# Row maxima in a clustered-attention and mixture-of-experts kernel: full-length passes over two thirds of the queries replaced by a maximum from PSUM and folds over all queries

## The chip, the cores and the metric

One NeuronCore of one Trainium2 chip. The metric is the device time of one execution in microseconds (us); lower is better. Three executions of the kernel before took 465.91, 466.88 and 467.42 us, median 466.88 us.

## What is computed

Two stages on one core. First an attention with a cluster mask: 2 batches, 8 heads, 768 tokens, 64 values per head. Every query and every key is assigned to the nearest of 16 centroids of its head (by cosine), and a query sees only keys of its own cluster:

```python
mask = q_assign[:, :, :, None] == k_assign[:, :, None, :]
scores = np.where(mask, scale * (q @ k.T), -1e9)
scores = scores - np.max(scores, axis=-1, keepdims=True)
attn = np.exp(scores) / (np.sum(np.exp(scores)) + 1e-9)
out = attn @ v
```

Then a mixture of 8 experts on the 2 x 768 tokens of 512 values that come out of it: a router picks one expert per token (a token can also keep the expert of the token before it), and the expert is two products with a relu between them, `p[e] * (relu(x @ w1[e]) @ w2[e])`.

The row maximum, `np.max(scores, axis=-1)`, is the part that the change edits.

## The kernel before, in words

The 16 (batch, head) combinations are handled one after the other; two heads of one batch make a pair u. For each head the kernel needs the 768 x 768 masked scores twice. The first time (function `stC`, queries on partitions) serves only to find each query's maximum. The maximum then goes as an extra column into the tile Q2, which one DMA transposes into Q2T (`fin`), and the second time (function `stD`, keys on partitions) the score product takes it off by itself, so that ScalarE can exponentiate the PSUM tile at once (L360, tile `e`, 32-bit). The exponentials are used as a 16-bit upper half and a 16-bit remainder `lo`; the remainder is a subtraction of two SBUF operands, seven times a head on GpSimd (L365) and twice on VectorE (L371). Products with the values follow (L388 to L390), then the division (`nm1`, L399 to L402; `nm2`, L410 on GpSimd).

A head's row-maximum stage consists of nine units. A unit is two matmuls (L318) that make a PSUM tile of 2 query tiles of 128 x 256 keys: `qp` is the pair of query tiles (0 to 2) and `kc` the third of the keys (0 to 2). `UORD` gives the order of the nine. There are two PSUM buffers for these tiles. In the kernel before,

- units with qp of 0 or 1 (two thirds of the queries) are copied by ScalarE as 16-bit data into the SBUF tile `ev` (L321), 128 x 512 each, six a head;
- units with qp of 2 are reduced by VectorE straight from PSUM into `mx` (L323), three a head;
- the four rows of `ev`, 768 keys each, are passed over by VectorE with an instruction that multiplies by 1 and gathers the maximum in its accumulator (L330; the profile shows it as TENSOR_SCALAR_CACHE_REDUCE and a DVE_READ_ACCUMULATOR);
- `fin` joins the three partial maxima of the last third (L336), writes them to Q2 (L338, L339) and issues the transposing DMA on SP's queue (L340).

The order of the work is written out by hand in one loop over steps `n` (L1114). In each step it emits one unit of the row maxima, 16 steps ahead (`c = n + LEAD`), one score tile, the pieces of the row maxima that are due by the table `OFFS`, the VectorE remainder and the value product of earlier tiles, and then whatever other tasks are due: loads, splits into 16-bit halves (L207, L213, L223) and cluster assignment (L252 to L267) of later pairs, routing, and the splits of the first expert's weights (L859, L861). Nine steps make a head. The entries of `OFFS` are (steps after the head's first unit, piece): pieces 0 to 3 are the passes over `ev`, piece 4 is `fin`:

```python
for off, what in OFFS:
    m = c - (off if c > 10 else min(off, 8))
    if 0 <= m < 9 * NH and m % 9 == 0:
        if what < 4:
            cs_[m // 9][1][what]()
        else:
            ins = cs_.pop(m // 9)[2]().ins
```

A scheduler turns this into each engine's own in-order queue, with the order of emission as priority, and sets the semaphores. The first batch's routing and the first expert's products run inside the later heads; the other experts follow after attention.

Of the kernel before, what the change touches and what calls it, by code (L numbers as in the profile page):

```python
# [36 lines left out]
NEQ = 2  # L37
NEM = 99
UORD = [(0, 0), (0, 1), (2, 0), (0, 2), (1, 0), (2, 1), (1, 1), (1, 2), (2, 2)]
OFFS = ((4, 0), (9, 1), (9, 2), (9, 3), (9, 4))  # L40
# [26 lines left out]
def tile_kernel(ctx, tc, q, k, v, centroids, w_gate, w_local, w1, w2, out):  # L67
# [43 lines left out]
    # constants  # L111
# [187 lines left out]
    # row maxima of head g: most units leave PSUM through ScalarE and are reduced as 16-bit data  # L299
    def stC(g):  # L300
# [3 lines left out]
        NEV = NEQ + (g % NEM == NEM - 1)  # L304
        NQ = 2 * NEV

        def unit(n):
            qp, kc = order[n]

            def f():  # L310
                if n == 0:
                    st["m"] = smp.tile([128, T], F32, name="m", tag="m", bufs=3)
                    st["mx"] = smp.tile([128, T, 3], F32, name="mx3", tag="mx3", bufs=3)
                    st["ev"] = smp.tile([128, 2 * NEV, 768], BF16, name="ev", tag="ev", bufs=EVB)
# [5 lines left out]
                if qp < NEV:  # L320
                    A.activation(out=st["ev"][:, 2 * qp:2 * qp + 2, kc * 256:kc * 256 + 256], in_=ps, func=AF.Copy)  # L321
                else:
                    mark["V"] = V.tensor_reduce(out=st["mx"][:, 2 * qp:2 * qp + 2, kc], in_=ps, axis=AX.X, op=ALU.max).ins  # L323
            return f

        def tree(i):
            e = st["ev"]
            for j in ((0, 1), (2, 3), (4, 5), ())[i]:
                if j < 2 * NEV:
                    mark["V"] = V.tensor_scalar(out=e[:, j], in0=e[:, j], scalar1=1.0, scalar2=None, op0=ALU.mult, op1=ALU.max, accum_out=st["m"][:, j:j + 1]).ins  # L330

        def fin():
            m = st["m"]
            q2 = rg(Q2, u)[:, hh]
            if NEV < 3:
                V.tensor_reduce(out=m[:, 2 * NEV:T], in_=st["mx"][:, 2 * NEV:T], axis=AX.X, op=ALU.max)  # L336
# [4 lines left out]
        return [unit(n) for n in range(9)], [lambda i=i: tree(i) for i in range(4)] if NQ else [], fin  # L341
# [226 lines left out]
    def lead(psp):  # L568
# [18 lines left out]
        # the first CAP_A of them come first, the rest with those of the next batch  # L587
# [8 lines left out]
    def unslot(pt, p, n, nm):  # L596
        """token indices of slots (0 where the slot is empty) for the gather and the scatter"""
# [17 lines left out]
    def lead_index(b, psp, tag=TX):  # L615
        """place of the leading expert's tokens of batch b, from 1; 0 for the others"""
# [46 lines left out]
    def plan(psp, tag):  # L663
        """ranks of the experts by their number of tokens, and each token's slot"""
# [20 lines left out]
        # index of each token among its expert's, its place in the block and the block  # L685
# [23 lines left out]
        # slot table: (place, block) <- token  # L709
# [23 lines left out]
        def over():  # L733
            """the slot table of the tokens past the static capacities, and the expert of each of its blocks"""
            c9 = tmp("c9", [128, E, E])
            n8 = tmp("n8", [128, E])
            # the key holds the number of tokens exactly
# [19 lines left out]
            # first block past the capacity, and capacity, of each token's expert  # L757
# [20 lines left out]
            # a token within the capacity has no block here  # L778
# [38 lines left out]
    def prio(d):  # L817
        """trace with a priority later by d"""
# [9 lines left out]
    def wload(r, kind, reg):  # L828
        """the loads and splits of the r-th expert's w1 (kind 0) or w2 (kind 1): pairs of steps"""
# [35 lines left out]
    def slot_blocks(cap):  # L865
        """blocks of slots: full ones of 128, whose output comes token-major, and a rest of up to 191"""
        nf = cap // 128
        if 0 < cap - nf * 128 < 64 and nf:
            nf -= 1
        return nf, cap - nf * 128  # L870
# [9 lines left out]
    def expert(r, cap, src, gi, sci, pr, mp, nbuf, g1pool=None, last=False, gates=None, putm=None):  # L880
        """gather, products and scatter of `cap` slots; gi, sci, pr give block i's column"""
        st = {"t": 0.0}

        def gate(t):
            """the next t us of this expert's products wait their turn behind the routing of the other batch"""
# [375 lines left out]
```

## Time and profile before

| | |
|---|---|
| median of three executions | 466.88 us |
| profiled execution: span from first to last instruction | 463.1 us |
| what lies around the span, by the three executions | 2.8 to 4.3 us |
| VectorE busy | 359.7 us, 78% |
| TensorE busy | 372.7 us, 80% |
| ScalarE busy | 264.6 us, 57% |
| GpSimd busy | 195.1 us, 42% |

In the profile PE is TensorE, DVE is VectorE, ACT is ScalarE, POOL is GpSimd and SP is SyncE. L330 is line 330 of the kernel before. A row of a list of instructions reads: line, engine, operation, tile written <- tiles read, shapes (partitions x elements and type), number of them | busy us in all, mean ns of one | idle us of the engine just before them, and what ended that idle time. Attention fills the span up to about 275 us, the experts the rest. Busy shares over the whole span mix these stages, so they are to be read stage by stage.

### The profile page before, as it was taken

To read this page: it belongs to the slowest core of one execution; us is meant where nothing else is said; L and a number is where in the kernel's file an instruction comes from. 1 tells how busy PE (TensorE), PEld (TensorE's weight loads), DVE (VectorE), ACT (ScalarE), POOL (GpSimd) and SP (SyncE) were. 2 spreads that over 40 slices of the span, in tenths; PEclk is the share of its full clock that TensorE was granted. 3 is DMA by queue.
4 is the path that set the end of the run, shared out by engine and by line. 5 is a ranking of instruction groups with operands and counts; after the bars stand their busy time and mean duration, and the time that the engine had idled before them with its cause. 6 is when DMAs were issued, how large, how long until landed. Compare 5 with 4: busy or idle time off the path is not lost. (4 is left out here: it accounts for less than half of the span.)

```text
span 463.1 us, 13303 instructions
## 1 busy us (share of the span) xinstructions
PE 372.7 (80%) x5315; PEld 315.7 (68%) x5315; DVE 359.7 (78%) x872; ACT 264.6 (57%) x493; POOL 195.1 (42%) x192
## 2 busy tenths in 40 slices
PE   0267697779788887988776699699999799999991
PEld 0246586668667775777665597498798597897870
DVE  7789999898989999989999338676685666566630
ACT  4277467667567875766776340145573765566430
POOL 3005447385647665656767631503233132201121
PEclk9998899898989999899999599899999899999997
DMA  8889889967967957237654601999699699697501
GB/s 191 120 192 205 248 124 223 213 134 178 171 154 159 152 116 119 47 82 147 151 169 128 124 8 33 259 282 245 194 347 324 191 313 314 212 281 240 183 31 33
DMA packets 125215, 81.48 MB, mean 176 GB/s; under 512 B 94537, under 2 KB 110153, under 8 KB 125152
## 3 DMA queue, kind: packets, MB, share of 16 engines
q1 hardware_dynamic: 122448, 73.47, 67.5%
q0 software_dynamic: 2704, 7.15, 4.4%
q8 instruction: 42, 0.69, 0.6%
q14 instruction: 21, 0.17, 0.1%
HBM read 47.04 MB, written 8.63 MB: 120 GB/s over the span
## 5 line engine op out<-in xcount | busy, mean ns | idle before, releaser
L365 POOL TENSOR_TENSOR lo<-e 128x512 f16<-128x512 f32 x112 | 129.1, 1171 | 97.3 <-ACT e L360 96.5
L360 ACT ACTIVATE e<-pst 128x512 f32<-128x512 f32 x144 | 82.1, 603 | 22.4 <-PE pst L358 18.4
L861 DVE SCALAR_TENSOR_TENSOR W<-wst,W 128x1024 f16<-128x1024 f32 x64 | 79.9, 1255 | 17.6 <-ACT W L859 17.4
L390 PE MATMUL o<-VH,lo 128*128 128x65 f16 x576 | 72.2, 197 | 16.9 <-DVE lo L371 15.8
L358 PE MATMUL pst<-Q2T,K2T 128*128 128x256 f16 x288 | 72.4, 289 | 7.5 <-DMA Q2T<-Q 7.5
L915 PE MATMUL g<-XT,W 128*128 128x200 f16 (+8 forms) x288 | 71.4, 259 | 7.5 <-DVE H L919 4.7
L357 PE MATMUL pst<-Q1T,K1T 128*128 128x256 f16 x288 | 76.0, 286 | 0.1
L318 PE MATMUL pm<-K2T,QMT 128*128 128x256 f16 x288 | 55.5, 291 | 23.5 <-DVE mx L323 18.1
L389 PE MATMUL o<-VL,e 128*128 128x64 f16 x576 | 74.4, 196 | 0.0
L388 PE MATMUL o<-VH,e 128*128 128x65 f16 x576 | 73.9, 198 | 0.0
L321 ACT ACTIVATE ev<-pm 128x512 bf16<-128x512 f32 x96 | 56.0, 599 | 28.2 <-PE pm L318 27.6
L916 PE MATMUL g<-XT,W 128*128 128x200 f16 (+8 forms) x288 | 71.5, 260 | 0.0
L859 ACT ACTIVATE W<-wst 128x1024 f16<-128x1024 f32 x64 | 66.9, 1052 | 5.8 <-DMA wst<-in_moe_w_dram 5.7
L390 PEld LDWEIGHTS <-lo 128*128 128x128 f16 x576 | 55.2, 100 | 22.1 <-DVE lo L371 19.2
L917 PE MATMUL g<-XT,W 128*128 128x200 f16 (+8 forms) x288 | 69.8, 260 | 0.0
L330 DVE TENSOR_SCALAR_CACHE_REDUCE ev<-ev 128x768 bf16<-128x768 bf16 x64 | 58.1, 943 | 0.1
L388 PEld LDWEIGHTS <-e 128*128 128x128 bf16 x576 | 55.5, 100 | 2.1 <-issue 0.2
L389 PEld LDWEIGHTS <-e 128*128 128x128 bf16 x576 | 55.5, 101 | 1.6
L918 ACT ACTIVATE H<-g 128x200 f16<-128x200 f32 (+8 forms) x72 | 24.3, 344 | 55.7 <-PE g L917 54.1
L919 DVE SCALAR_TENSOR_TENSOR H<-g,H 128x200 f16<-128x200 f32 (+8 forms) x72 | 25.9, 373 | 30.9 <-ACT H L918 30.3
L926 POOL DMA_INDIRECT out_dram<-ob,scim x16 | 18.3, 1146 | 71.0 <-ACT ob L924 30.5
L318 PEld LDWEIGHTS <-QMT 128*128 128x128 f16 x288 | 24.2, 103 | 30.4 <-issue 22.5
(298 smaller groups left out, 900.8 us busy)
## 6 DMA issues: line engine op xcount, KB each, us to landing
wst<-in_moe_w_dram SPq DMA_DIRECT2D x64, 512.0 KB, 5.4
xd<-xt SPq DMA_DIRECT2D x12, 384.0 KB, 3.6
ld_k<-in_k_dram SPq DMA_DIRECT2D x7, 384.0 KB, 4.7
ld_q<-in_q_dram SPq DMA_DIRECT2D x7, 384.0 KB, 5.0
ld_v<-in_v_dram SPq DMA_DIRECT2D x7, 384.0 KB, 4.5
Q1T<-QXT SPq DMA_DIRECT2D x14, 192.0 KB, 4.2
ld_k<-in_k_dram SPq DMA_DIRECT2D x2, 192.0 KB, 2.3
ld_q<-in_q_dram SPq DMA_DIRECT2D x2, 192.0 KB, 2.4
```

What stands on the lines that cost most here:

```text
L318: PE.matmul(out=ps[:, i], lhsT=rg(QMT, u)[:, hh * T + 2 * qp + i, :], rhs=rg(K2T, u)[:, hh * T + 2 * kc:hh * T + 2 * kc + 2, :], start=Tru ...
L357: PE.matmul(out=ps[:, i], lhsT=rg(K1T, u)[:, j, :], rhs=rg(Q1T, u)[:, hh * T + 2 * qc:hh * T + 2 * qc + 2, :], start=True, stop=False)
L358: PE.matmul(out=ps[:, i], lhsT=rg(K2T, u)[:, j, :], rhs=rg(Q2T, g)[:, 2 * qc:2 * qc + 2, :], start=False, stop=True)
L360: mark["A"] = A.activation(out=e, in_=ps.rearrange("p a b -> p (a b)"), func=AF.Exp, scale=SCL).ins
L365: G.tensor_tensor(out=lo, in0=e, in1=eh, op=ALU.subtract)
L388: PE.matmul(out=o[:, t, 0:65], lhsT=eh[:, sl], rhs=vh[:, hh, j, 0:65], start=first, stop=False, skip_group_check=True)
L389: PE.matmul(out=o[:, t, 0:64], lhsT=eh[:, sl], rhs=vl[:, hh, j, :], start=False, stop=False, skip_group_check=True)
L390: PE.matmul(out=o[:, t, 0:65], lhsT=lo[:, sl], rhs=vh[:, hh, j, 0:65], start=False, stop=False, skip_group_check=True)
L861: V.scalar_tensor_tensor(out=l[:, cs], in0=s[:, cs], scalar=WS, in1=h[:, cs], op0=ALU.mult, op1=ALU.subtract)
L915: PE.matmul(out=ps, lhsT=lh, rhs=XT[:, 2 * kk, 0:cap], start=(kk == 0), stop=False)
L916: PE.matmul(out=ps, lhsT=lh, rhs=XT[:, 2 * kk + 1, 0:cap], start=False, stop=False)
L917: PE.matmul(out=ps, lhsT=ll, rhs=XT[:, 2 * kk, 0:cap], start=False, stop=(kk == KD - 1))
```

## The change

All queries are now treated alike. ScalarE copies the units of the first two thirds of the keys (kc of 0 and 1) for all six query tiles into `ev`, which becomes 6 x 512 values in place of 4 x 768. A unit of the last third (kc of 2) is not reduced: VectorE takes, element by element, the maximum of its PSUM tile and of the copied first third, and writes it over that third in `ev`. Then `ev` is folded in halves by three element-wise maxima of two SBUF operands, 512 to 256 to 128 to 64 values a row, and one reduction of 6 x 64 values gives all six maxima. `mx` and the join of its parts are gone. The pieces are emitted 9, 10, 11 and 12 steps after the head's first unit, where half of the passes were emitted 4 steps after it and the other half 10; `fin` stays at 13. The order of the units stays, so that VectorE's units are now those at places 3, 7 and 8 of nine (counted from 0), where they were 2, 5 and 8.

```diff
-NEQ = 2
-NEM = 99
-OFFS = ((4, 0), (9, 1), (9, 2), (9, 3), (9, 4))
+OFFS = ((9, 0), (9, 1), (9, 2), (9, 3), (9, 4))
...
-                    st["mx"] = smp.tile([128, T, 3], F32, name="mx3", tag="mx3", bufs=3)
-                    st["ev"] = smp.tile([128, 2 * NEV, 768], BF16, name="ev", tag="ev", bufs=EVB)
+                    st["ev"] = smp.tile([128, T, 512], BF16, name="ev", tag="ev", bufs=EVB)
...
-                if qp < NEV:
-                    A.activation(out=st["ev"][:, 2 * qp:2 * qp + 2, kc * 256:kc * 256 + 256], in_=ps, func=AF.Copy)
+                ev = st["ev"][:, 2 * qp:2 * qp + 2]
+                if kc < 2:
+                    A.activation(out=ev[:, :, kc * 256:kc * 256 + 256], in_=ps, func=AF.Copy)
                 else:
-                    mark["V"] = V.tensor_reduce(out=st["mx"][:, 2 * qp:2 * qp + 2, kc], in_=ps, axis=AX.X, op=ALU.max).ins
+                    mark["V"] = V.tensor_tensor(out=ev[:, :, 0:256], in0=ps, in1=ev[:, :, 0:256], op=ALU.max).ins
             return f

-        def tree(i):
+        def fold(w):
             e = st["ev"]
-            for j in ((0, 1), (2, 3), (4, 5), ())[i]:
-                if j < 2 * NEV:
-                    mark["V"] = V.tensor_scalar(out=e[:, j], in0=e[:, j], scalar1=1.0, scalar2=None, op0=ALU.mult, op1=ALU.max, accum_out=st["m"][:, j:j + 1]).ins
+            mark["V"] = V.tensor_tensor(out=e[:, :, 0:w], in0=e[:, :, 0:w], in1=e[:, :, w:2 * w], op=ALU.max).ins
+
+        def last():
+            mark["V"] = V.tensor_reduce(out=st["m"], in_=st["ev"][:, :, 0:64], axis=AX.X, op=ALU.max).ins

         def fin():
...
-            if NEV < 3:
-                V.tensor_reduce(out=m[:, 2 * NEV:T], in_=st["mx"][:, 2 * NEV:T], axis=AX.X, op=ALU.max)
...
-        return [unit(n) for n in range(9)], [lambda i=i: tree(i) for i in range(4)] if NQ else [], fin
+        return [unit(n) for n in range(9)], [lambda: fold(256), lambda: fold(128), lambda: fold(64), last], fin
```

In both kernels the order of the units (qp, kc) is

```python
UORD = [(0, 0), (0, 1), (2, 0), (0, 2), (1, 0), (2, 1), (1, 1), (1, 2), (2, 2)]
```

## Rows read from the trace of the kernel before

**Rows 1.** The head of the profile's page: span, and of each engine busy us, share of the span and number of instructions.

```profile
span 463.1 us, 13303 instructions
...
PE 372.7 (80%) x5315; PEld 315.7 (68%) x5315; DVE 359.7 (78%) x872; ACT 264.6 (57%) x493; POOL 195.1 (42%) x192
```

**Rows 2.** Busy time by stretch. Columns: the stretch, its length, busy us and number of instructions of PE, PEld, DVE, ACT and POOL, granted TensorE clock, share of the DMA engines, GB/s.

```profile
67.00:239.00 172.00, 141.58 (x2375) 120.38 (x2372) 162.30 (x358) 120.93 (x238) 109.56 (x95) 0.96 0.73 149
...
239.00:275.00 36.00, 27.64 (x424) 23.54 (x421) 22.63 (x60) 17.28 (x33) 21.93 (x20) 0.86 0.37 87
```

**Rows 3.** VectorE's instructions in the stretch from 67 to 239 us, grouped by line and shape, costliest first.

```profile
L330 DVE TENSOR_SCALAR_CACHE_REDUCE ev<-ev 128x768 bf16<-128x768 bf16 x48 | 43.5, 943 | 0.1
L323 DVE TENSOR_REDUCE mx<-pm 128x2 f32<-128x512 f32 x37 | 25.3, 683 | 4.5 <-PE pm L318 4.4
L371 DVE TENSOR_TENSOR lo<-e 128x512 f16<-128x512 f32 x24 | 23.6, 984 | 0.1
...
L207 DVE SCALAR_TENSOR_TENSOR K<-ld_k,K 128x384 f16<-128x384 f32 x8 | 6.9, 894 | 0.0
L207 DVE SCALAR_TENSOR_TENSOR QX<-ld_q,QX 128x384 f16<-128x384 f32 x8 | 6.6, 868 | 0.1
L207 DVE SCALAR_TENSOR_TENSOR VL<-ld_v,VH 128x384 f16<-128x384 f32 x9 | 6.4, 709 | 0.0
L861 DVE SCALAR_TENSOR_TENSOR W<-wst,W 128x1024 f16<-128x1024 f32 x4 | 6.0, 1528 | 0.0
...
L259 DVE TENSOR_TENSOR eq<-eq,iota 128x384 f16<-128x384 f16 x5 | 3.7, 740 | 0.0
L267 DVE TENSOR_TENSOR oh<-eq,gm 128x384 f16<-128x384 f16 x5 | 3.6, 714 | 0.0
...
L213 DVE COPY QM<-QX 128x768 f16<-128x768 f16 x5 | 3.0, 593 | 0.0
L213 DVE COPY K<-K 128x768 f16<-128x768 f16 x5 | 2.8, 553 | 0.8 <-DMA K2T<-K 0.8
...
L223 DVE COPY Q<-QX 128x768 f16<-128x768 f16 x5 | 2.6, 526 | 1.6 <-DMA Q2T<-Q 1.6
...
L336 DVE TENSOR_REDUCE m<-mx 128x2 f32<-128x6 f32 x12 | 1.8, 150 | 0.1
```

**Rows 4.** GpSimd's instructions in the same stretch, grouped in the same way.

```profile
L365 POOL TENSOR_TENSOR lo<-e 128x512 f16<-128x512 f32 x83 | 97.1, 1188 | 50.5 <-ACT e L360 49.9 <-DVE m L336 0.4
L410 POOL TENSOR_TENSOR xt<-xf,xt 128x384 f16<-128x384 f32 x12 | 13.0, 1080 | 11.8 <-ACT xt L406 11.8
```

**Rows 5.** Who waited for whom in the same stretch: engine, tile and line that waited <- what it waited for: us in all, times, longest us.

```profile
PE pm L318 <- DVE mx L323: 11.2, 13, 2.6
...
DVE mx L323 <- PE pm L318: 4.4, 6, 1.3
```

**Rows 6.** VectorE's instructions in order of time from 146 to 149 us: start us, duration us, engine, line, operation, tiles and shapes.

```profile
146.30 0.94 DVE L330 TENSOR_SCALAR_CACHE_REDUCE ev<-ev 128x768 bf16<-128x768 bf16 x1
...
147.17 0.94 DVE L330 TENSOR_SCALAR_CACHE_REDUCE ev<-ev 128x768 bf16<-128x768 bf16 x1
...
148.04 0.68 DVE L323 TENSOR_REDUCE mx<-pm 128x2 f32<-128x512 f32 x1
```

**Rows 7.** VectorE's instructions from the start of the span to 36 us, before GpSimd's first L365 (at 36.7 us), grouped by line and shape.

```profile
L207 DVE SCALAR_TENSOR_TENSOR K<-ld_k,K 128x384 f16<-128x384 f32 x4 | 2.2, 556 | 1.6 <-ACT K L215 1.6
...
L252 DVE TENSOR_REDUCE mx<-sim 128x24 f32<-128x384 f32 x1 | 0.6, 558 | 0.9 <-PE sim L247 0.9
L256 DVE TENSOR_TENSOR eq<-sim,mx 128x384 f16<-128x384 f32 x1 | 0.6, 558 | 0.0
L267 DVE TENSOR_TENSOR oh<-eq,gm 128x384 f16<-128x384 f16 x1 | 0.6, 557 | 0.1
L263 DVE TENSOR_REDUCE gm<-eq 128x24 f16<-128x384 f16 x1 | 0.6, 552 | 0.0
...
L259 DVE TENSOR_TENSOR eq<-eq,iota 128x192 f16<-128x192 f16 x2 | 0.5, 258 | 0.1
...
L213 DVE COPY K<-K 128x768 f16<-128x768 f16 x1 | 0.4, 360 | 1.5 <-DMA K2T<-K 1.5
L259 DVE TENSOR_TENSOR eq<-eq,iota 128x384 f16<-128x384 f16 x1 | 0.4, 359 | 0.0
```

**Rows 8.** Single lines over the whole span: number, shortest, median and longest duration in ns, first and last start in us, shapes.

```profile
L330 DVE TENSOR_SCALAR_CACHE_REDUCE ev<-ev x64: 910/943/953, 27.3 to 252.3; 128x768 bf16<-128x768 bf16 x64
...
L402 DVE TENSOR_TENSOR xf<-o,r x16: 541/547/558, 67.6 to 274.3; 128x384 f32<-128x384 f32 x16
...
L371 DVE TENSOR_TENSOR lo<-e x32: 646/691/1552, 42.4 to 267.5; 128x512 f16<-128x512 f32 x32
...
L259 DVE TENSOR_TENSOR eq<-eq,iota x9: 257/359/1122, 16.9 to 207.3; 128x384 f16<-128x384 f16 x7, 128x192 f16<-128x192 f16 x2
...
L365 POOL TENSOR_TENSOR lo<-e x112: 1032/1040/2022, 36.7 to 269.2; 128x512 f16<-128x512 f32 x112
```

**Rows 9.** VectorE and GpSimd in order of time from 63 to 67 us (rows of the other engines left out).

```profile
63.17 2.69 POOL L365 TENSOR_TENSOR lo<-e 128x512 f16<-128x512 f32 x2 [1.78 <-ACT e L360]
...
63.73 1.23 DVE L267 TENSOR_TENSOR oh<-eq,gm 128x384 f16<-128x384 f16 x1
64.89 1.52 DVE L371 TENSOR_TENSOR lo<-e 128x512 f16<-128x512 f32 x1
```

More of the change, by code (lines that the diff above doesn't have):

```diff
@@ L303, in stC @@
         order = UORD
-        NEV = NEQ + (g % NEM == NEM - 1)
-        NQ = 2 * NEV
         def unit(n):
@@ L1129, in tile_kernel @@
                     if what < 4:
-                        if cs_[m // 9][1]:
-                            cs_[m // 9][1][what]()
+                        cs_[m // 9][1][what]()
                     else:
```

## The prediction

> **What bounds the kernel now.** First the page's engine totals [rows 1]: no engine is busy over the whole span, so the whole-span shares decide nothing. I then cut the span [rows 2]. From 67 to 239 us, twelve heads of attention run (L336, once a head, stands there 12 times, [rows 3]), so a head takes 172 / 12 = 14.3 us. In that stretch VectorE is busy 162.3 of 172 us, 94%, against 82% for TensorE, 70% for ScalarE and 64% for GpSimd. From 239 to 275 us VectorE is busy only 22.6 of 36 us. So in the attention stretch VectorE's queue sets the pace, and it is the queue that the change edits. The idle times say the same: GpSimd stands idle 49.9 us because ScalarE's exponentials come late [rows 4], and TensorE waits 11.2 us for VectorE to empty the PSUM tiles of the row maxima, while VectorE's own longest wait, for those tiles' matmuls, is 4.4 us [rows 5].
>
> Next, what VectorE spends [rows 3]. Row maxima cost, per head, four L330 passes, three L323 reductions and one L336. The passes are 943 ns each in the list, but one starts 0.87 us after the other [rows 6], because the start of an instruction overlaps the end of the one before by some 70 ns. I count in such start-to-start times.
>
> **What goes.** Four passes at 0.87 us are 3.48 us; L336 (150 ns listed) is 0.08 us. Together 3.56 us a head, all on the bounding queue.
>
> **What stays the same.** ScalarE evicts six 128x512 tiles a head before (two thirds of the queries, all keys) and six after (all queries, two thirds of the keys). The three remaining tiles were reduced from PSUM (683 ns) and now enter a maximum with a 16-bit SBUF operand. With both in their undisturbed state, before GpSimd starts, a two-operand instruction with one operand in PSUM takes what a reduction of the same 384 columns takes, 558 ns each (L256, L252, [rows 7]). So the three cost the same, 0. Its new wait, for ScalarE's copy of an earlier unit, is free: units 3, 7 and 8 need units 0, 4 and 2, and with two PSUM buffers the matmuls of unit n+2 cannot begin before unit n has been emptied. The tile for the copies has the same size (4x768 and 6x512 values), and the transposing DMA of Q2T is issued at the same step, so SP's queue is moved past nothing. GpSimd gets no instruction and loses none.
>
> **What comes.** Three folds and a reduction. The 16-bit two-operand L259 takes 258 ns for 192 columns and 359 ns for 384 [rows 7], so 0.526 ns a column and some 157 ns fixed. The folds write 6x256, 6x128 and 6x64 columns: 965, 561 and 359 ns. The last reduction reads 384 columns: 552 ns (L263). Less 70 ns each, 0.90 + 0.49 + 0.29 + 0.48 = 2.16 us. Bare saving: 3.56 - 2.16 = 1.40 us a head.
>
> **The price that is not in the list: GpSimd.** The removed pass has one SBUF input and never varies, 910 to 953 ns with GpSimd busy 64% of the time; L402, with one input in PSUM, keeps to 541 to 558 ns. L371, with two SBUF inputs, runs from 646 to 1552 ns around a median of 691, and L259 up to 1122 ns [rows 8]. The timeline shows what it waits for [rows 9]: L267 at 63.73 takes 1.23 us (557 ns undisturbed) because GpSimd's L365 began at 63.17; GpSimd's second L365 then ends at 65.86 and the L371 that follows takes 1.52 us. So each of the three folds, with two SBUF inputs, can be held by a running L365, and the removed passes could not. Bounds for the wait of one fold: 0 (none running) and 1.03 us (a whole L365, its minimum, [rows 8]). Over the stretch, means less undisturbed times [rows 3, 7, 8]: L371 24 x 0.29, L207 25 x 0.26, L259 5 x 0.38, L267 5 x 0.16, the copies L213 and L223 15 x 0.20: 19.3 us on 74 instructions, 0.26 us each. I take 0.30, L371's value, since it is the commonest and also stands behind other such work. Three folds: 0.90 us.
>
> The Trainium skill, on the page SBUF — State Buffer, section "Who interferes with whom", states this as a rule: a VectorE instruction with two SBUF inputs contends with a GpSimd instruction that reads SBUF, the accumulating form of tensor_scalar does not take the shared ports, and the loser of the lock blocks fully. By that rule the trace agrees (1552 ns against 953); it speaks against this change, and reckoned without it the sum would be the bare saving of 1.40 us.
>
> **Two smaller terms.** The folds hold GpSimd in turn, so it is late and meets the other such instructions more often: 6 a head, by a tenth of their 0.26 us or a little less, +0.1 us (bounds 0 and, doubled, 0.3). The tiles that VectorE empties move from units 2, 5, 8 to 3, 7, 8: two lie side by side, and TensorE, with two buffers, waits for both. Bounds: from -0.37 us (VectorE's 4.4 us of waits for these matmuls vanish) to +0.93 us (TensorE's whole 11.2 us comes through once more), per head; +0.1, near zero, as VectorE rarely runs dry [rows 5].
>
> **Sum.** -1.40 + 0.90 + 0.10 + 0.10 = -0.30 us a head. It counts for 14 of the 16 heads; at the last one VectorE has slack [rows 2]. -4.2 us. For the first head nothing hides latency: all folds now stand behind the last unit, 2.16 us, where two passes and L336 did, 1.82 us: +0.3 us (bounds 0 and +0.6). Total -3.9 us. Everything behind attention (routing, the experts) hangs on its end and moves along. The profiled span is 463.1 us; the executions that were timed lie 2.8 to 4.3 us above it, their median 3.8. 463.1 - 3.9 + 3.8 = **463.0 us**, against the median of 466.88. VectorE stays the bound, at some 94%.
>
> **Rivals.**
> *The lock hardly bites.* Folds may fall where GpSimd waits for exponentials (it is idle over a third of the stretch). At a wait of 0.08 us the head gains 0.96 us, 14 heads 13 us: 454 us; the bare end is 449. Against it: the mean of 74 instructions.
> *No change.* The shared access counts as a resource of its own. Undisturbed, the instructions named above and the four L861 hold it 46.6 us of the stretch, 3.9 us a head; GpSimd's L365 (83 x 1.03) and L410 98.7 us, 8.2 a head [rows 3, 4, 8]. With the folds' 1.89 us that is 14.0 of 14.3 us. If each holds it for its listed time, a head cannot shrink, as the waits grow until the gain is used up: 466.5 us. Against it: the L371 above ended 0.55 us after L365 did, less than its 0.69, so it is held for less.
> *Slower: a convoy.* A fold holds GpSimd up; the L365 that then stands waiting starts when the fold ends, and the next fold, if it follows at once, waits for all of it. With GpSimd wanted 64% of the time, the second and third fold wait 0.64 x 1.03 = 0.66 us each: 1.62 us in place of 0.90, +0.42 us a head, 14 heads +5.9: 473 us; with every one of them caught, 1.16 us a head and 483. The point from which it decides: 0.40 us a fold. For it: the timeline has two in a row both waiting [rows 9]. Against it: the folds are put one step apart, with other work between.
> *The folds run at one column a cycle* (the change doesn't do what it says): L263's 552 ns for 384 columns against L259's 359. Doubles the folds' columns, +1.4 us a head, +15 us: 482. Against it: L259 has the same kinds of operands, in rows too.
>
> **Chances.** Forecast 0.38, little lock 0.12: faster 0.50. No change 0.17. Convoy 0.25, slow folds 0.08: slower 0.33. What a measurement of this kernel tells from no change is about 0.3%, 1.4 us. The likeliest case itself spans 459 to 465.4 us. The range for 8 in 10, 454 to 475, reaches from the little-lock case to just past the middle of the convoy and leaves out the slow folds and both far ends.
>
> **What would show it.** Right: three fold groups at medians near 965, 561 and 359 ns with means some 0.3 us above; the PSUM maximum at 0.69 us without spread; VectorE's busy time down by some 5 us and its share of the stretch still near 94%; L365's mean a little above 1188 ns. Wrong: fold means 0.5 us or more above their medians (convoy); fold medians twice the ones above (one column a cycle); folds as computed but VectorE's idle time grown by what was saved, with TensorE or Q2T named in front of it.

## The result: 1.1% slower, where a small gain was forecast

The changed kernel takes **472.96 us** (median of 4 executions, 471.98 to 473.62), the kernel before, run beside it, 466.39 us (464.25 to 467.42): a ratio of 1.0114, 95% interval 1.0073 to 1.0156. The forecast was 463.0 us and faster. The measured time lies in the range, near the 473 us of the convoy rival, but the folds' waits are not of the size which that rival needs, as shown below.

The profiled execution took 471.98 us, its span 469.9 us. Its page answers to [rows 1]:

```profile
span 469.9 us, 13272 instructions
...
PE 374.1 (80%) x5315; PEld 317.2 (68%) x5315; DVE 359.2 (76%) x792; ACT 260.3 (55%) x493; POOL 207.6 (44%) x192
```

VectorE runs 80 instructions fewer and is busy as long as before (359.7 us). GpSimd, with the same 192 instructions, is busy 12.5 us longer. Next the busy time by stretch, with the columns of [rows 2]. 67 to 245 us holds the last reductions (L328) of twelve heads, as 67 to 239 us held twelve joins (L336) before; 20 us to the last head's first normalisation step holds the row maxima of all heads. First the changed kernel, then the kernel before, whose stretch ends at 273.9 us:

```profile
20.00:280.70 260.70, 203.46 (x3276) 171.52 (x3274) 228.00 (x423) 164.29 (x331) 161.68 (x129) 0.93 0.69 145
67.00:245.00 178.00, 141.75 (x2382) 121.03 (x2382) 166.06 (x303) 120.29 (x242) 120.71 (x97) 0.94 0.67 138
```

```profile
20.00:273.90 253.90, 201.19 (x3244) 168.80 (x3242) 227.60 (x499) 167.43 (x330) 147.90 (x129) 0.94 0.73 149
```

The two windows, 178 and 172 us, are not the time of twelve heads to the microsecond: thirteen of L334, which comes once a head, start in the longer one. Marks that come once a head count better. These are the first step that ends a head's row maxima (L334, before L338) and the first normalisation step (L395, before L399), over the whole span (number, shortest, median and longest ns, first and last start in us), after and then before:

```profile
L334 DVE TENSOR_SCALAR Q<-m x16: 168/487/3212, 36.1 to 260.6; 128x6 f16<-128x6 f32 x16
...
L395 DVE TENSOR_SCALAR r<-o x16: 148/152/165, 62.5 to 280.7; 128x6 f32<-128x6 f32 x16
```

```profile
L338 DVE TENSOR_SCALAR Q<-m x16: 163/182/1015, 32.1 to 256.6; 128x6 f16<-128x6 f32 x16
...
L399 DVE TENSOR_SCALAR r<-o x16: 146/153/166, 60.3 to 273.9; 128x6 f32<-128x6 f32 x16
```

From the first head to the last the row maxima take 224.5 us in both kernels, 14.97 us a head; the normalisation takes 14.55 us a head against 14.24. So a head costs 0 to 0.3 us more, depending on the mark, where -0.30 was forecast. Head 0's maxima come 4.0 us later. Attention ends 6.8 us later (280.7 against 273.9 us). What comes behind takes 189.2 us in both traces, so the whole loss is made in attention. There VectorE's busy time is unchanged (228.0 and 227.6 us), its idle time rises from 26.3 to 32.7 us, and GpSimd is busy 13.8 us longer.

VectorE's groups over the whole span, 16 heads (line, operation, tiles and shapes, count, busy us, mean ns, idle time before). They answer to [rows 3]; L320 is the maximum from PSUM, L325 the three folds, L328 the last reduction, L334 the first step that ends a head, L367 VectorE's remainders, L265 the one-hot product:

```profile
L367 DVE TENSOR_TENSOR lo<-e 128x512 f16<-128x512 f32 x32 | 33.7, 1053 | 2.2 <-ACT e L356 2.1
L320 DVE TENSOR_TENSOR ev<-pm,ev 128x512 bf16<-128x512 f32 x48 | 32.5, 685 | 5.7 <-PE pm L314 4.3 <-ACT ev L318 1.0
L325 DVE TENSOR_TENSOR ev<-ev 128x1536 bf16<-128x1536 bf16 x16 | 19.8, 1235 | 1.0 <-DVE ev L320 0.5
L325 DVE TENSOR_TENSOR ev<-ev 128x768 bf16<-128x768 bf16 x16 | 14.6, 912 | 0.2
L325 DVE TENSOR_TENSOR ev<-ev 128x384 bf16<-128x384 bf16 x16 | 12.1, 754 | 0.1
L334 DVE TENSOR_SCALAR Q<-m 128x6 f16<-128x6 f32 x16 | 10.9, 681 | 0.2
L328 DVE TENSOR_REDUCE m<-ev 128x6 f32<-128x384 bf16 x16 | 8.7, 542 | 0.2
...
L265 DVE TENSOR_TENSOR oh<-eq,gm 128x384 f16<-128x384 f16 x7 | 6.8, 969 | 0.1
```

And GpSimd's remainders, over the whole span, after and then before:

```profile
L361 POOL TENSOR_TENSOR lo<-e 128x512 f16<-128x512 f32 x112 | 142.7, 1296 | 96.1 <-ACT e L356 95.3 <-PE o L386 0.5
```

```profile
L365 POOL TENSOR_TENSOR lo<-e 128x512 f16<-128x512 f32 x112 | 129.1, 1171 | 97.3 <-ACT e L360 96.5 <-DVE m L336 0.4
```

The same 112 subtractions take 125 ns more each, 14.0 us in all: the folds hold GpSimd back as it holds them. Over the whole span of before, the four groups that compare were L371 952 ns, L338 340, L267 765 and L323 684.

How the waits stack up shows at the last head. VectorE's rows from its last PSUM instruction to the end of the head's maxima (start us, duration us, engine, line, operation, tiles), with rows left out, first before:

```profile
250.24 0.68 DVE L323 TENSOR_REDUCE mx<-pm 128x2 f32<-128x512 f32 x1
...
251.44 0.94 DVE L330 TENSOR_SCALAR_CACHE_REDUCE ev<-ev 128x768 bf16<-128x768 bf16 x1
...
252.30 0.94 DVE L330 TENSOR_SCALAR_CACHE_REDUCE ev<-ev 128x768 bf16<-128x768 bf16 x1
...
255.28 0.14 DVE L336 TENSOR_REDUCE m<-mx 128x2 f32<-128x6 f32 x1
...
256.60 0.18 DVE L338 TENSOR_SCALAR Q<-m 128x6 f16<-128x6 f32 x1
```

and after:

```profile
249.79 0.68 DVE L320 TENSOR_TENSOR ev<-pm,ev 128x512 bf16<-128x512 f32 x1
...
250.59 1.22 DVE L857 SCALAR_TENSOR_TENSOR W<-wst,W 128x1024 f16<-128x1024 f32 x1
251.72 0.95 DVE L325 TENSOR_TENSOR ev<-ev 128x1536 bf16<-128x1536 bf16 x1
...
252.89 1.23 DVE L367 TENSOR_TENSOR lo<-e 128x512 f16<-128x512 f32 x1
254.05 1.39 DVE L325 TENSOR_TENSOR ev<-ev 128x768 bf16<-128x768 bf16 x1
...
257.43 1.19 DVE L325 TENSOR_TENSOR ev<-ev 128x384 bf16<-128x384 bf16 x1
258.54 1.52 DVE L367 TENSOR_TENSOR lo<-e 128x512 f16<-128x512 f32 x1
...
260.06 0.53 DVE L328 TENSOR_REDUCE m<-ev 128x6 f32<-128x384 bf16 x1
260.62 3.21 DVE L334 TENSOR_SCALAR Q<-m 128x6 f16<-128x6 f32 x1
```

and GpSimd's under its end:

```profile
260.88 2.05 POOL L361 TENSOR_TENSOR lo<-e 128x512 f16<-128x512 f32 x2
...
262.87 0.92 POOL L406 TENSOR_TENSOR xt<-xf,xt 128x384 f16<-128x384 f32 x1
```

From the maximum's end at 250.47 to the end of L334 at 263.83 a chain of some 2.6 us of undisturbed work takes 13.4 us. Other work stands between its links on VectorE's queue, the second and third fold wait 0.83 us each, and L334, which undisturbed takes 168 ns, ends when three GpSimd instructions have ended. Before, the same way took 5.9 us (250.92 to 256.78).

The units are hardly late: head 0's last one ends at 30.5 us, before at 29.8, and the last head's 0.4 us earlier than before. But the end of the last head's maxima comes 7.1 us later, and attention ends 6.8 us later: in these two traces the whole loss stands between the last head's last unit and the end of its maxima. Behind them ScalarE's exponentials wait for their score tile, up to 10.0 us at a time (who waited for what, us in all, times, longest us; after from 250 to 281 us, then before from 250 to 274 us):

```profile
ACT e L356 <- PE pst L354: 12.2, 6, 10.0
```

```profile
ACT e L360 <- PE pst L358: 1.9, 4, 0.8
```

At the other heads the way from the last unit to the end of the maxima grows as well, from 4.5 us in the mean of 16 heads to 8.8 us, but there the work of the next heads goes on beside it.

### The profile page after: what moved, and what is told of

It is laid out like the page before. It is cut to its first block, busy times and chain, and to the rows that moved or that the text cites. A ratio compares the mean times of both kernels' runs of the same rounds, so it can differ in the third digit from the quotient of the medians.

```text
span 469.9 us, 13272 instructions
## 1 busy us (share of the span) xinstructions
PE 374.1 (80%) x5315; PEld 317.2 (68%) x5315; DVE 359.2 (76%) x792; ACT 260.3 (55%) x493; POOL 207.6 (44%) x192
## 5 line engine op out<-in xcount | busy, mean ns | idle before, releaser
L361 POOL TENSOR_TENSOR lo<-e 128x512 f16<-128x512 f32 x112 | 142.7, 1296 | 96.1 <-ACT e L356 95.3
L356 ACT ACTIVATE e<-pst 128x512 f32<-128x512 f32 x144 | 80.9, 604 | 33.8 <-PE pst L354 28.4
L386 PE MATMUL o<-VH,lo 128*128 128x65 f16 x576 | 69.7, 197 | 14.4 <-DVE lo L367 10.1
L911 PE MATMUL g<-XT,W 128*128 128x200 f16 (+8 forms) x288 | 72.2, 262 | 6.7 <-DMA XT<-xg 3.8
L912 PE MATMUL g<-XT,W 128*128 128x200 f16 (+8 forms) x288 | 72.3, 262 | 0.3 <-issue 0.3
L384 PE MATMUL o<-VH,e 128*128 128x65 f16 x576 | 72.3, 197 | 0.0
L385 PE MATMUL o<-VL,e 128*128 128x64 f16 x576 | 72.2, 195 | 0.0
L913 PE MATMUL g<-XT,W 128*128 128x200 f16 (+8 forms) x288 | 70.5, 262 | 0.0
L922 POOL DMA_INDIRECT out_dram<-ob,scim x16 | 16.8, 1050 | 73.4 <-ACT ob L920 36.9
L325 DVE TENSOR_TENSOR ev<-ev 128x1536 bf16<-128x1536 bf16 (+2 forms) x48 | 46.4, 967 | 1.3 <-DVE ev L320 0.5
```

What stands on the lines that cost most here:

```text
L356: mark["A"] = A.activation(out=e, in_=ps.rearrange("p a b -> p (a b)"), func=AF.Exp, scale=SCL).ins
L361: G.tensor_tensor(out=lo, in0=e, in1=eh, op=ALU.subtract)
L384: PE.matmul(out=o[:, t, 0:65], lhsT=eh[:, sl], rhs=vh[:, hh, j, 0:65], start=first, stop=False, skip_group_check=True)
L385: PE.matmul(out=o[:, t, 0:64], lhsT=eh[:, sl], rhs=vl[:, hh, j, :], start=False, stop=False, skip_group_check=True)
L386: PE.matmul(out=o[:, t, 0:65], lhsT=lo[:, sl], rhs=vh[:, hh, j, 0:65], start=False, stop=False, skip_group_check=True)
L911: PE.matmul(out=ps, lhsT=lh, rhs=XT[:, 2 * kk, 0:cap], start=(kk == 0), stop=False)
```

## The experiments

Ratios are to the kernel before, run beside it on the same chip. Their intervals reach about 0.3 to 0.7% to either side, so two ratios must differ by some 0.5 to 0.9% to be told apart. "Lock" is short for VectorE and GpSimd waiting for each other.

**Is it the start of the folds, or the order of units?** x1_late, in the kernel before: `OFFS = ((4, 0), (9, 1), ...)` becomes `((9, 0), (9, 1), ...)`, the change's own edit of that constant. x5_head0, in the changed kernel, computes head 0 in the old way (`OLD = g == 0`). x7_before_head0new, in the kernel before, computes head 0 alone in the new way. x8_uord, in the changed kernel, puts the units in natural order:

```
-UORD = [(0, 0), (0, 1), (2, 0), (0, 2), (1, 0), (2, 1), (1, 1), (1, 2), (2, 2)]
+UORD = [(0, 0), (0, 1), (0, 2), (1, 0), (1, 1), (1, 2), (2, 0), (2, 1), (2, 2)]
```

> The kernel before with one part of the change alone: its passes over ev are all emitted behind the last unit (steps 9 and 10 in place of 4 and 10). Theory lock (the folds, with two SBUF inputs, wait for GpSimd and make others wait; the saving is eaten): the passes have one input, so this costs little, 465 to 468 us against 466.4. Rival late (what costs is that nothing of a head's maximum is done before its last unit, so Q2T is late): most of the change's +6.6 us appears here, 470 us or more.

> The changed kernel, with head 0 alone done in the old way (passes and reductions, its first passes at step 4). In the trace of the changed kernel head 0's maxima come 4.0 us later than before (36.1 against 32.1 us), since VectorE's queue puts other instructions between the links of its chain of folds. Theory start (this delay reaches the end): 466 to 469 us where the changed kernel has 473. Theory lock alone (the loss comes head by head later): 471 us or more.

> The kernel before, with head 0 alone done in the new way (maximum from PSUM, three folds, reduction). Theory start: 3 to 6 us longer than before, though GpSimd has no work yet and no fold can wait for it. Theory lock alone: the same as before within 1.5 us.

> The changed kernel with the units in natural order, so that VectorE's units stand at places 2, 5 and 8 as before, not at 3, 7 and 8. Theories start and lock: 471 to 475 us, as the changed kernel. Rival units (two of VectorE's units side by side stall TensorE): 470 us or less.

x1_late: 466.57 us, 0.9978 [0.9952, 1.0005]. It left the order of every engine's queue as it was, so this part of the change does nothing by itself. x5_head0: 477.53 us, 1.0227 [1.0180, 1.0273], slower still, although head 0's maxima were ready at 31.6 us in place of 36.1; an early start did not win the time back. x8_uord: 473.23 us, 1.0152 [1.0106, 1.0198]; VectorE's units in their old places did not win it back either. x7_before_head0new was the surprise: 474.37 us, 1.0133 [1.0087, 1.0179]. One head of 16 computed anew costs the kernel before as much as the whole change. That is past the 3 to 6 us that the start theory gave for it, while x5_head0 speaks against that theory, so the start is not settled by these two. (x7_before_head0new also gives `mx` one buffer in place of three; in its trace and in that of the kernel before, each head's three reductions come behind the join of the head before, so nothing is seen to wait for it.) Such an edit also gives every engine's queue a new order, because the scheduler deals the queues out by priorities over the whole program.

**What does a new order alone cost?** Three edits of the kernel before that keep every instruction and change only the order: y1_before_u378 (units reordered so that VectorE's come at 3, 7 and 8), y2_before_kp24 and y4_before_lov36:

```
-KP = 28
+KP = 24
```

```
-LOV = (2, 6)
+LOV = (3, 6)
```

> The kernel before with its units in another order, so that VectorE's three reductions stand at places 3, 7 and 8, as VectorE's maxima do in the changed kernel. Same instructions, same number; the scheduler deals out another order on every engine. Theory order (the order that the scheduler dealt out for the kernel before happens to be a good one, and any edit that deals again loses it): 470 to 476 us. Theory lock: no two-input work is added, so 466 to 469 us. Rival units (the places 3, 7, 8 are bad by themselves): 470 us or more here and 466 to 469 in the next.

> The kernel before with the splits and transposes of later pairs emitted four steps later (KP 24 in place of 28), a change of order alone. Theory order: 470 to 476 us. Theory lock: 466 to 469 us.

> The kernel before with VectorE's two remainders of a head taken from score tiles 3 and 6 in place of 2 and 6; same instructions, another order on every engine. Theory order: 470 to 476 us. Theory lock: 466 to 469 us.

468.98 us, 475.78 us and 477.49 us: ratios 1.0035 [0.9996, 1.0074], 1.0159 [1.0118, 1.0201] and 1.0222 [1.0158, 1.0286]. So an order alone is worth up to 2.2%, twice the loss to be explained. All three are above the kernel before (the first not clear of none), and so is k_before_lead18 below (1.0133); the kernel before is a favourable order among these.

**The change under other orders.** If the order were the whole cause, the change should not lose when both kernels get the same new constants. y3_after_kp24 and y5_after_lov36 are the changed kernel with the two edits above; k_before_lead18 and k_after_lead18 have a third:

```
-LEAD = 16
+LEAD = 18
...
-P2 = -7.5
-P1 = -23.0
-L2P = -5.0
-VP = -7.0
+P2 = -9.5
+P1 = -25.0
+L2P = -7.0
+VP = -9.0
```

With LEAD 18 a pair's values are written over those of the pair three before it up to two steps early, so the last two of nine products of the second head of five pairs take other values; instructions and sizes are the same.

> The changed kernel with the same change of order (KP 24). Theory order: as often better as worse than the changed kernel, 469 to 476 us, and by no more than 2 us longer than the kernel before this edit was also made to. Theory lock: 5 us or more longer than the kernel before with KP 24.

> The changed kernel with VectorE's remainder subtractions of a score tile at tiles 3 and 6 in place of 2 and 6 (LOV), beside y4_before_lov36 that measured 477.5. Theory order: 472 to 479, no longer than y4_before_lov36. Theory lock: 482 or more, the 5 to 6 us of the change on top of y4_before_lov36.

> The kernel before with LEAD 18 in place of 16, and the places P1, P2, L2P and VP that are counted from it moved by -2, so that a head's projections and the rest start two steps earlier against its scores: the same instructions on every engine, in another order. Theory order (the 466 of the kernel before is a favourable order among its neighbours): 468 to 478, as with three reorderings already run (469.0, 475.8, 477.5). Theory lock (the loss is the change's own, the order matters little): 464 to 469.

> The changed kernel with the same five constants. Theory order: within 3 us of k_before_lead18 on either side. Theory lock: 5 us or more longer than k_before_lead18.

**The lock taken out.** x3_after_quiet and x4_before_quiet replace GpSimd's subtraction, in the changed kernel and in the kernel before, by an instruction that reads nothing; both then leave out the remainder of seven score tiles in nine:

```
-                    G.tensor_tensor(out=lo, in0=e, in1=eh, op=ALU.subtract)
+                    G.memset(lo, 0.0)
```

> The changed kernel with GpSimd's seven subtractions a head replaced by writing zeros into lo (it leaves out the remainder of seven in nine score tiles); GpSimd then reads no SBUF there. To be compared with the next kernel, the same edit to the kernel before. Theory lock: the folds drop to about 965, 561 and 359 ns each, VectorE saves the bare 1.4 us a head, and this kernel is 8 to 20 us shorter than the next. Rival (late, or units): it stays 4 us or more longer than the next.

> The kernel before with GpSimd's seven subtractions a head replaced by writing zeros into lo (the same part left out). Both theories: shorter than before, because VectorE's own two-input instructions (0.26 us each, 6 a head) no longer wait: 14 heads x 1.6 us, 440 to 455 us. Its passes keep to 910 to 953 ns.

**The folds replaced by one reduction.** x2_onered, in the changed kernel, reads all 6x512 values with one instruction that has one SBUF input and runs beside GpSimd:

```
-            mark["V"] = V.tensor_reduce(out=st["m"], in_=st["ev"][:, :, 0:64], axis=AX.X, op=ALU.max).ins
+            mark["V"] = V.tensor_reduce(out=st["m"], in_=st["ev"], axis=AX.X, op=ALU.max).ins
...
-        return [unit(n) for n in range(9)], [lambda: fold(256), lambda: fold(128), lambda: fold(64), last], fin
+        return [unit(n) for n in range(9)], [last, lambda: None, lambda: None, lambda: None], fin
```

The same two lines make x6_onered_head0 from x5_head0, x2_kp24 from y3_after_kp24, z_onered_lead18 from k_after_lead18 and x2_quiet from x3_after_quiet.

> The changed kernel with its three folds and last reduction replaced by one reduction of 6 x 512 columns (3072 columns, about 3.28 us start to start, one SBUF input), emitted where the first fold was. Per head VectorE: 3.28 us against the 3.56 us of passes and L336 that went. Theory lock: nothing of it waits for GpSimd, so it comes out faster than before by 0.28 us a head, 462 to 465 us. Rival units (the maximum from PSUM, the new order of VectorE's units at 3, 7, 8, or the late start of the reduction cost the time): 469 us or more, as in the changed kernel.

> One reduction of 6 x 512 columns in place of the folds in heads 1 to 15, and head 0 done in the old way. Theory start: the single reduction saves 0.28 us a head and lost it again to its late first head (36.1 us there too), so this one is faster than before, 0.985 to 0.995 of it. Theory lock alone: as the single reduction everywhere, 1.00.

> One reduction of 6x512 in place of the folds, under KP 24, beside y3_after_kp24 (473.6) and y2_before_kp24 (475.8). Theory lock and theory chain: 3 to 10 us shorter than y3_after_kp24, 464 to 471. Theory order (the pairs differ by the deal of the queues alone): no sign, 468 to 480.

> The changed kernel with one reduction of 6x512 in place of three folds and the short reduction (no instruction with two SBUF inputs in the row maxima, some 18 us more bare VectorE work over 14 heads), with the constants of k_after_lead18. Theory lock: 3 to 8 us shorter than k_after_lead18, as x2_onered was 5 us shorter than the changed kernel. Theory order: no sign to be foretold, within 6 us of k_after_lead18 either way; shorter than the kernel before's 466 would make it a version that beats both.

> One reduction of 6x512 in place of the three folds and the short reduction, and GpSimd's subtraction replaced by a memset of 0 as in x3_after_quiet (it leaves out the remainder e - e16 of 7 of 9 score tiles). Theory lock (the folds lose by their waits for GpSimd alone): with nothing to wait for the folds are the cheaper ones, so this is 0 to 8 us longer than x3_after_quiet's 449.6, against 5 us shorter with GpSimd's subtraction in. Theory chain (four links in a row on VectorE's queue, each with a wait for the one before and with other work between, delay a head's maxima whatever GpSimd does): 3 to 8 us shorter than x3_after_quiet.

What was measured in the last three groups, side by side (median us, ratio to the kernel before, interval):

| same constants | kernel before | changed kernel | folds replaced by one reduction |
|---|---|---|---|
| as they are | 1 | 472.96, 1.0114 [1.0073, 1.0156] | 467.76, 0.9995 [0.9967, 1.0023] |
| KP 24 | 475.78, 1.0159 | 473.61, 1.0112 [1.0067, 1.0156] | 471.30, 1.0086 [1.0046, 1.0126] |
| LEAD 18 | 470.94, 1.0133 [1.0077, 1.0190] | 476.42, 1.0219 [1.0163, 1.0276] | 466.77, 1.0021 [0.9991, 1.0051] |
| LOV (3, 6) | 477.49, 1.0222 | 481.89, 1.0368 [1.0309, 1.0428] | not run |
| head 0 in the old way | as they are | 477.53, 1.0227 | 474.64, 1.0163 [1.0122, 1.0204] |
| no GpSimd subtraction | 445.14, 0.9499 [0.9459, 0.9540] | 449.61, 0.9599 [0.9559, 0.9639] | 449.93, 0.9590 [0.9521, 0.9659] |

*Column two to three.* With the subtraction in, the change costs +1.14, -0.47, +0.86 and +1.46%: on average +0.75%, 3.5 us, with a scatter of 0.85% between pairs and one sign the other way; four such pairs do not put the mean clear of zero. Each theory missed: the order theory at y5_after_lov36, which came at 481.89 us, at the lock theory's 482, and at k_after_lead18, 5 us behind its partner; the lock theory at y3_after_kp24, 2 us ahead of its partner, and at three of the four reorderings of the kernel before, for which it gave 464 to 469 us. No pair alone gives the change's own cost: each carries that and what the order happens to do to it, which is as large.

*Column three to four.* One reduction is shorter than the folds every time GpSimd subtracts: -1.19, -0.26, -1.98 and, with head 0 in the old way, -0.64%. The second and the fourth are too small to be told from none by themselves. Without the subtraction the difference is gone (-0.09%). This is what the lock theory gave and not the 3 to 8 us of the chain theory (four links lose whatever GpSimd does). It is one pair, though, known to 0.8%, and the four differences beside it scatter by 0.7%, so the times alone do not decide it. Not all forecasts were met: x2_onered came at 467.76 us, between the lock theory's 462 to 465 and the 469 or more of its rival, x6_onered_head0 at 1.0163, where one theory gave 0.985 to 0.995 and the other 1.00, and under KP 24 and LEAD 18 the single reduction gains 2.3 and 9.7 us, where 3 to 10 and 3 to 8 were given.

VectorE's rows under x3_after_quiet and x2_onered (whole span, same columns as above) do show what each pays:

```profile
L325 DVE TENSOR_TENSOR ev<-ev 128x1536 bf16<-128x1536 bf16 x16 | 15.2, 952 | 0.3
L325 DVE TENSOR_TENSOR ev<-ev 128x768 bf16<-128x768 bf16 x16 | 8.8, 552 | 0.1
L328 DVE TENSOR_REDUCE m<-ev 128x6 f32<-128x384 bf16 x16 | 8.7, 545 | 0.1
L325 DVE TENSOR_TENSOR ev<-ev 128x384 bf16<-128x384 bf16 x16 | 5.9, 370 | 0.1
L334 DVE TENSOR_SCALAR Q<-m 128x6 f16<-128x6 f32 x16 | 3.2, 197 | 0.1
```

```profile
L328 DVE TENSOR_REDUCE m<-ev 128x6 f32<-128x3072 bf16 x16 | 53.5, 3344 | 0.4
```

Unlocked, the folds and the short reduction take 952 + 552 + 370 + 545 = 2.42 us a head; locked, 1235 + 912 + 754 + 542 = 3.44 us, as much as the single reduction's 3.34 us. The folds' whole advantage over it is eaten by waits here; under KP 24 the folds and the short reduction take 3.13 us and under LEAD 18 3.51. GpSimd's row separates them: under the folds its subtraction takes 1296 ns (as is), 1240 (KP 24) and 1225 (LEAD 18); under the single reduction

```profile
L361 POOL TENSOR_TENSOR lo<-e 128x512 f16<-128x512 f32 x112 | 127.0, 1158 | 86.6 <-ACT e L356 86.2
```

and 1163 and 1184 ns, which is where the kernel before stands (1171, 1144, 1149).

*The last row of the table* speaks to the forecast's main step, and against the lock as the whole cause: with GpSimd's subtraction gone, the changed kernel is still 4.5 us longer than the kernel before with the same edit. The lock theory gave 8 to 20 us shorter, its rival 4 us or more longer. Busy time from 20 us to the last head's first normalisation step, in x4_before_quiet, x3_after_quiet and x2_quiet:

```profile
20.00:248.10 228.10, 192.00 (x3210) 163.90 (x3211) 191.67 (x498) 162.94 (x327) 71.18 (x123) 0.94 0.84 166
```

```profile
20.00:255.70 235.70, 194.52 (x3233) 166.03 (x3234) 170.42 (x420) 164.05 (x329) 73.75 (x123) 0.92 0.82 161
```

```profile
20.00:259.00 239.00, 199.03 (x3233) 167.46 (x3230) 186.21 (x370) 165.83 (x328) 72.35 (x123) 0.92 0.79 158
```

Without the lock the change does give VectorE 21.2 us back (191.67 to 170.42 us), 1.3 us a head, close to the bare saving of 1.40. The stretch grows by 7.6 us all the same, and VectorE's idle time goes from 36.4 to 65.3 us. The single reduction, 15.8 us busier than the folds, has a stretch 3.3 us longer and ends at the same total time. (Of these two kernels the execution in the profile is the longest, 2 to 3 us above the median.) So VectorE's busy time is not what the length follows here, where VectorE is busy 84% of the stretch to begin with.

With the subtraction in, VectorE is busy 4.7 us less under KP 24, 7.4 under LEAD 18 and 7.8 under LOV (3, 6) over the whole span (365.3 to 360.6, 368.7 to 361.3 and 364.8 to 357.0 us), about what was forecast, and the times go by -0.47, +0.86 and +1.46%. The stretches of y4_before_lov36 and y5_after_lov36, 7.7 us less VectorE work in 7.2 us more time (3.7 us of which come back behind it):

```profile
20.00:281.60 261.60, 207.56 (x3256) 173.34 (x3255) 232.72 (x499) 165.08 (x329) 147.14 (x129) 0.91 0.71 144
```

```profile
20.00:288.80 268.80, 206.21 (x3263) 173.86 (x3264) 224.97 (x421) 166.14 (x331) 155.91 (x129) 0.91 0.68 141
```

**How long a head's maxima take.** In every pair the way from a head's last unit to the end of its maxima gets longer (end of VectorE's third PSUM instruction of a head to the end of L338 or L334, mean of 16 heads): from 4.5 to 8.8 us as they are, 4.5 to 8.6 under KP 24, 4.2 to 8.4 under LEAD 18, 4.9 to 9.2 under LOV (3, 6), and 2.6 to 7.3 without GpSimd's subtraction. One reduction takes 7.5, 7.4, 7.2 and, without the subtraction, 6.7 us. So most of this growth is there without the lock: the whole reduction now stands behind the last unit. At the last head no later head's work hides it; there it goes from 5.9 to 13.4, 5.2 to 12.1, 4.6 to 9.0, 8.8 to 7.0 and 3.3 to 11.0 us, in the same order. In all but the LOV pair the last head's last unit itself comes between 5.6 us earlier and 0.7 us later than in the kernel before, and what is lost is lost behind it; in the LOV pair it comes 4.7 us later. No run gave the last head alone the old way, so this is read from traces and not tested.

**A version that beats both?** None beat the kernel before by what can be measured. One reduction matches it (0.9995 and, under LEAD 18, where some products take other values, 1.0021), beats the changed kernel, and is 0.7 and 1.1% shorter than the kernel before under KP 24 and LEAD 18.

## Why the prediction was wrong

**What held.** The PSUM maximum takes 685 ns, without spread, as L323 did. The folds' undisturbed times were put at 965, 561 and 359 ns and are 952, 552 and 370; the last reduction at 552 and is 542 to 545. The waits of the three folds were put at 0.90 us a head and are 0.28 + 0.36 + 0.38 = 1.02 (locked means less those of x3_after_quiet). The rule from the Trainium skill, on the page SBUF — State Buffer, section "Who interferes with whom", holds for both kinds: two SBUF inputs wait; a tensor_reduce, which that section says never contends on trn2, takes 3344 ns in x2_onered and 3346 ns in x2_quiet. Everything behind attention moved along to 0.1 us.

**Step that failed first: "VectorE's queue sets the pace".** From a share of 94% the prediction concluded that what VectorE saves, the head saves. The trace says that it was busy, not that the others could go faster. When work was taken off it, its idle time grew by more: 28.9 us for 21.2 us without GpSimd's subtraction, and in the LOV pair 14.9 us for 7.7 us. What the waits in front of it name is a mixture: in x3_after_quiet, K2T's transpose 13.3 us, the exponentials 11.4, Q2T 5.9, matmuls and others the rest. Most of these were there in x4_before_quiet; K2T's grew by 10.1 us (x3_after_quiet, then x4_before_quiet):

```profile
L211 DVE COPY K<-K 128x768 f16<-128x768 f16 x7 | 3.8, 540 | 13.3 <-DMA K2T<-K 13.3
```

```profile
L213 DVE COPY K<-K 128x768 f16<-128x768 f16 x7 | 3.6, 521 | 3.2 <-DMA K2T<-K 3.2
```

The prediction had listed this as a sign of being wrong, and gave it no chance.

**Step that failed second: what hides latency, and the smaller terms.** The sum let the change count at 14 of 16 heads: at the last one "VectorE has slack", which put that head at 0, and the first one's later maxima at +0.3 us, bounds 0 and 0.6. Measured: the last head's maxima end 7.1 us later, though its last unit does not come later, and head 0's come 4.0 us later. Slack in VectorE's busy time did not shorten a chain of four instructions that each wait for the one before and for GpSimd.

"The folds hold GpSimd in turn" was put at +0.1 us a head, bound 0.3. GpSimd's own part of it was the larger: its subtraction grew by 14.0 us, 0.87 us a head, and by 8 to 11 us under KP 24, LEAD 18 and LOV (3, 6). Of VectorE's other instructions the remainders grew by 101 ns x 32 = 3.2 us, the step that ends a head by 341 ns x 16 = 5.5 us (3.0 of them at the last head) and the one-hot products by 204 ns x 7 = 1.4 us; others shrank, L207's splits of K by 2.0 us. All of VectorE's instructions outside the row maxima together take 6.0 us more, 0.37 us a head; under KP 24 it is +5.6, under LEAD 18 -2.2, under LOV (3, 6) -0.6 us. So the term itself held on average, and what it took to be its price was elsewhere. L338's 340 ns mean for six values a partition, which stood in the trace before, was overlooked: it is such a waiting instruction, at the very place where the head's result leaves.

**Step that failed third: order cost nothing.** An edit of 16 heads' row maxima gives each engine a new queue order. Nothing in the text priced that; reorderings of the kernel before cost 0.35 (not clear of none) to 2.2%.

**An error of reading.** "The folds are put one step apart, with other work between" stood as evidence against the convoy. The second number in `OFFS` is the piece, not a step: all four and the end of the head are emitted at step 9, and not at 9 to 12 and 13, as the description of the change has it too (nor the second half of the passes before at 10). The other work between them that the timeline shows was put there by the scheduler. The convoy needed 0.40 us a fold; measured are 0.34, so it did not decide. That the time is the one that it gave is chance.

**What stays open.** That waits for GpSimd eat what the folds save over one reduction is shown by their durations. That the time against one reduction follows from it is likely, by five pairs, and not shown; whether it works through GpSimd's later remainders or through VectorE's waits the runs did not separate. Why the changed kernel is slower than the kernel before is not shown. The lock is not the whole of it, since without the subtraction 1.0% is still lost, and so with the single reduction. Both share the PSUM maxima and a chain that starts only behind the last unit, and the traces put most of the loss behind that unit at the last head; but an order of queues is worth as much, and no run tells them apart.

## What to carry to other kernels

A queue that is 94% busy is not yet the bound: take work off it in an experiment and see whether the time follows, before counting a saving on it. Try the longer instruction that no other engine holds up beside shorter ones that can be held: in five comparisons here one reduction with one input was level with or ahead of three folds and a short one with 28% less undisturbed work. Look at the last item of a pipeline by itself: its chain is the one that nothing hides. Where a scheduler deals out the queues, time a change under several settings of its constants: one pair here said +1.1%, another -0.5%, and an edit that changed no instruction cost 2.2%.

## What was not expected of the hardware

A wait for GpSimd can fall on the smallest instruction, with one SBUF input. L334 writes six values a partition from a single SBUF input and takes 168 ns undisturbed; at the last head it took 3.21 us, from 260.62 us to just past the end of the L406 that GpSimd began at 262.87. Its mean is 681 ns in the changed kernel, 340 before (L338) and, with GpSimd's subtraction gone, 197 (x3_after_quiet) and 253 (x4_before_quiet). It is not the folds alone that bring this on: with the single reduction it is 536 ns, and under KP 24, LEAD 18 and LOV (3, 6) it is 537, 344 and 466 ns after against 428, 393 and 462 before. All ten of the changed kernel's and all four of the kernel before's that took over 250 ns began while a GpSimd instruction ran and ended 36 to 48 ns after the end of one. An instruction that only writes holds it too: in x4_before_quiet four of them took 406 to 528 ns and ended 34 to 36 ns after one of GpSimd's memsets. The waits of larger ones came in one size there: 1.39 - 0.56, 1.19 - 0.36 and 1.52 - 0.69 (L325 at 254.05 and 257.43, L367 at 258.54) are 0.83 us each.
